# Preparing raw float64 weights in pairs of units instead of one by one

## The chip, the cores and the metric

The kernel runs on one core of a Trainium2 chip. The metric is the device time of one execution in microseconds, as the median of three runs: 1222.59 us before the change (1215.45 to 1223.43).

## What is computed

An attention over 4 batches, 12 heads, 448 tokens and 64 channels, whose queries and keys are normalised per row, feeds two MLPs one after the other. All inputs arrive in float64 or float32; here the weights are read as 64-bit words.

```python
q_n, k_n = rmsnorm(q, g_q), rmsnorm(k, g_k)
attn = softmax(scale * q_n @ k_n.T)          # per batch and head
x = (attn @ v) -> [1792, 768]
x = (x @ w_a) * (x @ w_b) @ w_out            # 768 -> 1536 -> 768
h = x @ w_in                                 # 768 -> 2048
g = np.maximum(h, 0.0) + alpha * np.minimum(h, 0.0)
return g @ w2_out                            # 2048 -> 768
```

## The kernel before

**Stages.** The four batches go through four MLP stages each: `a` (products with w_a and w_b, 24 chains), `y` (w_out of the first MLP, 6 chains in two parts), `h` (w_in of the second, 16 chains) and `o` (w_out of the second, 6 chains in four parts). A hand-written list gives their order: a0 y0 h0 o0 a1 y1 a2 h1 o1 y2 h2 a3 o2 y3 o2 h3 o3. The attention of the next batches is a generator, `att_steps`, of which a few steps are taken at each tick of a stage; the attention of batch 0 runs first, in float32, with nothing to run beside it but the preparation of weights.

**Products.** Each float32 operand is held as a high and a low half in float16, and a product of 128 rows takes three matmuls (`prod`). A *unit* is what one weight tile serves: a chain, or a part of it, of six (a, y, h: 768 columns) or four (o: 512 columns) blocks, so 18 or 12 matmuls of 448 columns. The last o and y stages (o2, y3, o3; `FAST`) use seven formed products for eight, on half the tokens, with weights that `form_weights` combines beforehand from the stored halves through raw buffers and GpSimd's queue.

**Weights.** A list `stream` holds the units in the order of use. The first use of a weight (76 units, all in batch 0's stages) goes through four steps, which `advance` calls as the stream moves on:

- `w_load` (L748): DMA of the 64-bit words into a raw buffer, 12 units ahead of use;
- `w_convert` (L764 to L779), 8 ahead: a Prelu on ScalarE takes the upper words to float32, VectorE shifts (L767) and ORs the lower bits in (L770), ScalarE squares the result with a sum per row (L778);
- `w_scale`, 6 ahead: a matmul with ones (`total`) adds the sums over the partitions, and three small operations on VectorE (`power`) make a power of two as scale and its inverse. For a and h two chains share one such computation, with a scale for each; y takes two parts, o four;
- `w_split` (L831 to L835), 3 ahead: ScalarE writes the scaled high half, VectorE the residual, and SyncE's queue stores both in HBM.

Later uses of the same weight read the stored halves (L744), 4 units ahead; formed weights are read at L738, one unit further ahead. The pools: raw 5 buffers, wf (float32, and formed weights) 6, wh (halves) 5, each for one unit. Two raw buffers (`early`) serve the attention of batch 0 as its transposed queries and keys until that attention ends. `slot` has 35 buffers for activations: X, AB, Y and G. `tmp` has three.

**Order.** The program order gives priorities, and a list scheduler with a cost estimate orders each engine's instructions at build time; where the code says `keep_in_program_order`, that is fixed. Each engine then runs its list in order and waits on semaphores. A stage calls `next_w` (and so `advance`) between a unit's matmuls and the evacuation of its result. SyncE's queue takes in one line the loads of q, k, v and weights, the stores of halves and results, and the transposes of q, k and the probabilities (L355, L358, L490).

Of the kernel before, what the change touches and what calls it, by code (L numbers as in the profile page):

```python
# [19 lines left out]
def attention_gated_mlps_kernel(  # L20
# [24 lines left out]
    SLOTS = 35  # L45
# [25 lines left out]
    def slot32(name):  # L71
# [6 lines left out]
    kd0 = keep_p.tile([128, 2 * KB * D], F32, name="kd0")  # L78
# [15 lines left out]
    cgf = const.tile([128, KF2], F32, name="cgf")  # L94
# [8 lines left out]
        "a": const.tile([128, 2 * KF], F32, name="inv_a"),  # L103
        "y": const.tile([128, KD], F32, name="inv_y"),
        "h": const.tile([128, KF2], F32, name="inv_h"),
# [165 lines left out]
    def prep2f(g):  # L271
        d = P[g]
        kr, r = d["kr"], d["rk"]
        kd = kd0[:KP]
        d["kd"] = kd
        i = nc.vector.tensor_tensor(
            kd.rearrange("p (i h d) -> p h i d", i=KB, h=2),
            kr.rearrange("p (h i) d -> p h i d", h=2),
            r[:KP, NI:NS].rearrange("p (h i) -> p h i", h=2).unsqueeze(3).to_broadcast([KP, 2, KB, D]),
            op=ALU.mult,  # L280
        )
        if g == 0:
            tc.keep_in_program_order(i)
# [379 lines left out]
    def form_block(kind, i, j, cols):  # L663
# [3 lines left out]
        def raw():  # L667
            return raw_p.tile([128, 784], I64, tag="raw", name="raw")

        def load():  # L670
            d["x"] = x = raw().bitcast(F16)[:, 0:8 * w].rearrange("p (q l n) -> p q l n", q=4, l=2)
# [5 lines left out]
        def whole(q):  # L677
            if q == 0:
                d["r"] = raw().bitcast(F32)[:, 0:4 * w].rearrange("p (q n) -> p q n", q=4)
# [45 lines left out]

    def size(kind):
        return CHAINS[kind][2] * 128

    def w_load(u):
# [3 lines left out]
        if key[-1] == "s":  # L733
            kind, i, (f, j), _ = key
            t = wf_p.tile([128, 768], F32, tag="wf", name="ws").bitcast(F16)
            t = t[:, 0:2 * WIDE[kind]].rearrange("p (l n) -> p l n", l=2)
            tc.keep_in_program_order(
                nc.sync.dma_start(out=t, in_=form_source(kind, i, f, j))  # L738
            )
            w16[u] = t  # L740
            return
        if key in scratch:
            t = wh_p.tile([128, 2, 768], F16, tag="w16", name="w16")[:, :, 0:n]
            nc.sync.dma_start(out=t, in_=scratch[key])  # L744
            w16[u] = t
# [3 lines left out]
        if state["pin"]:  # L749
            tc.keep_in_program_order(i)  # L750
        raws[u] = t
        scratch[key] = hbm.tile([128, 2, n], F16, name=f"sc_{key[0]}{key[1]}_{key[2]}")

    def w_convert(u):
# [6 lines left out]
        t = wf_p.tile([128, 768], F32, tag="wf", name="wf")[:, 0:size(kind)]  # L761
# [12 lines left out]
        _, parts, _ = CHAINS[kind]  # L774
        j = (n * parts + part) % (parts * GROUP[kind])
        if j == 0:
            sums[0] = sm_p.tile([128, 4], F32, tag="ss", name="ss")
# [3 lines left out]
        if j == parts * GROUP[kind] - 1:  # L781
            squares[u] = sums[0][:, 0:j + 1]
# [3 lines left out]
    def w_scale(u):  # L786
# [4 lines left out]
        _, parts, _ = CHAINS[kind]  # L791
        chains = GROUP[kind]
        us = range(u - parts * chains + 1, u + 1)
        sc = sm_p.tile([128, 2], F32, tag="sc", name="sc")[:, 0:chains]
        iv = inv[kind][:, n - chains + 1:n + 1]
        power(total(squares.pop(u), len(us), chains), sc, iv, 2)
        for x in us:
            scales[x] = sc[:, (x - us[0]) // parts:(x - us[0]) // parts + 1]
        if (kind, n) == ("h", KF2 - 1):
# [22 lines left out]
    def junk(width, n):  # L822
        return jk_p.tile([128, width], BF16, tag="junk", name="junk")[:, 0:n]

    def w_split(u):
        if u not in scales:
            return
        t, s = wf.pop(u), scales.pop(u)
        n = t.shape[1]
        w = wh_p.tile([128, 2, 768], F16, tag="w16", name="w16")[:, :, 0:n]  # L830
# [5 lines left out]
        w16[u] = w  # L836


    STEPS = [(w_load, 12), (w_convert, 8), (w_scale, 6), (w_split, 3)]
# [4 lines left out]
    again = sorted(set(range(len(stream))) - set(firsts))  # L844
# [96 lines left out]

    def blocks():
        r = raw_p.tile([128, 784], I64, tag="raw", name="raw").bitcast(F32)
        r = r.rearrange("p (j n) -> p j n", j=7)
# [119 lines left out]
    def stage_a(b):  # L1064
        raw = {}
        for f in range(KF):
            for w in range(2):
                yield
                ps = new_ps()[:, 0:S]
                hw = unit()  # L1070
# [292 lines left out]
```

## Time and profile before

| | |
|---|---|
| median of three runs | 1222.59 us (1215.45, 1222.59, 1223.43) |
| profiled execution | 1215.08 us, span 1213.0 us |
| TensorE busy (matmul) | 1145.4 us, 94% |
| VectorE busy | 816.5 us, 67% |
| ScalarE busy | 770.1 us, 63% |
| mean granted TensorE clock | 0.98 |

The shares are means over stages with different limits: the attention of batch 0 and the preparation of weights lie in the first 440 us, while from 440 us on the weights come ready from HBM. Busy times by stretch say more. TensorE's busy time is modelled from pipelined matmuls; its idle time and what ended it are the better guide.

### The profile page before, as it was taken

Reading aid. Unit: us, or ns where it says so; the run is one execution under the profiler, and the core shown is the slowest. Engines: PE = TensorE matmul, PEld = TensorE weight load, DVE = VectorE, ACT = ScalarE, POOL = GpSimd, SP = SyncE. Lnnn points to the kernel's source line nnn. Section 1 sums busy time; section 2 is a strip of 40 time slices with the busy share of each in tenths; the row PEclk is TensorE's granted clock in tenths of the full one; section 3 lists DMA queues with packets and bytes.
Section 4 is the critical chain, followed back from the end, with each engine's and each line's share of the span. In section 5 each row is a group of like instructions: output and inputs, shape, how many; then the busy total and the mean of one; then the engine's idle time right before and its main releaser. Section 6 shows DMA issues by size and latency. Waiting matters only on the chain. (4 is left out here: it accounts for less than half of the span.)

```text
span 1213.0 us, 20078 instructions
## 1 busy us (share of the span) xinstructions
PE 1145.4 (94%) x7144; PEld 650.6 (54%) x7144; DVE 816.5 (67%) x1695; ACT 770.1 (63%) x1543; POOL 108.2 (9%) x176
## 2 busy tenths in 40 slices
PE   6997999899989799998999999999999999999997
PEld 3553554445434344444445554544555558996597
DVE  7898999999899666677754376554356677523631
ACT  7998999999899666767534366564255335513532
POOL 1000000000001000000012100122200562000000
PEclk9997999999989899998999999999999999999999
DMA  7658999999999999987985677898834798873465
GB/s 190 174 163 211 315 326 329 288 298 305 309 246 308 252 237 253 248 199 173 198 225 152 159 175 164 199 222 190 228 117 135 247 299 284 272 210 107 129 188 171
DMA packets 319267, 269.78 MB, mean 222 GB/s; under 512 B 178464, under 2 KB 275232, under 8 KB 319168
## 3 DMA queue, kind: packets, MB, share of 16 engines
q1 hardware_dynamic: 311376, 246.41, 75.9%
q0 software_dynamic: 7792, 22.10, 6.3%
q8 instruction: 56, 0.92, 0.3%
q14 instruction: 43, 0.35, 0.1%
HBM read 179.77 MB, written 43.25 MB: 184 GB/s over the span
## 5 line engine op out<-in xcount | busy, mean ns | idle before, releaser
L110 PEld LDWEIGHTS <-w 128*128 128x128 f16 x4104 | 398.2, 99 | 393.5 <-issue 39.6
L110 PE MATMUL p<-x,w 128*128 128x448 f16 x1728 | 336.3, 354 | 0.5 <-DVE ab L1080 0.4
L110 PE MATMUL p<-y,w 128*128 128x448 f16 x1152 | 221.6, 352 | 1.4 <-DVE t L1187 1.3
L110 PEld LDWEIGHTS <-ws 128*128 128x128 f16 x1386 | 132.5, 98 | 3.3 <-DMA ws<-f_o_S 2.7
L110 PE MATMUL p<-ab,w 128*128 128x448 f16 x648 | 129.7, 359 | 1.3 <-ACT ab L894 1.2
L110 PE MATMUL p<-g,w 128*128 128x448 f16 x576 | 119.8, 362 | 4.6 <-ACT g L1172 3.5
L421 DVE TENSOR_REDUCE nm<-s 128x2 f32<-128x896 f32 x84 | 91.2, 1086 | 33.5 <-PE s L110 33.3
L483 ACT ACTIVATE p<-pf,ri 128x448 f16<-128x448 f32 x126 | 81.8, 665 | 35.9 <-DMA pT<-p 27.4
L484 DVE SCALAR_TENSOR_TENSOR p<-pf,ri,p 128x448 f16<-128x448 f32 x126 | 84.6, 680 | 28.1 <-ACT p L483 28.0
L110 PE MATMUL l<-g,ws 128*128 128x224 f16 x960 | 94.2, 259 | 1.8 <-DMA ws<-f_o_S 1.8
L438 ACT ACTIVATE pf<-s,nm,esc 128x448 f32<-128x448 f32 x126 | 90.0, 719 | 1.4
L832 DVE SCALAR_TENSOR_TENSOR w<-wf,sc,w 128x768 f16<-128x768 f32 (+1 forms) x76 | 70.1, 929 | 2.5 <-ACT w L831 2.1
L831 ACT ACTIVATE w<-wf,sc 128x768 f16<-128x768 f32 (+1 forms) x76 | 65.4, 869 | 2.6 <-DMA sc_h<-w 1.7
L764 ACT ACTIVATE wf<-raw 128x768 f32<-128x768 f32 (+1 forms) x76 | 63.6, 843 | 5.2 <-DMA raw<-in_moe_w_out_dram 3.2
L770 DVE SCALAR_TENSOR_TENSOR wf<-raw,wf 128x768 int32<-128x768 int32 (+1 forms) x76 | 65.7, 868 | 0.3
L1083 ACT ACTIVATE junk<-ab 128x448 bf16<-128x448 f32 x48 | 27.6, 574 | 59.8 <-DVE ab L1080 59.6
L778 ACT ACTIVATE junk<-wf 128x768 bf16<-128x768 f32 (+1 forms) x76 | 59.3, 781 | 1.3 <-DVE wf L770 1.3
L707 POOL DMA_DIRECT2D f_o_S<-raw x48 | 33.8, 807 | 292.6 <-DVE raw L703 214.0
L110 PE MATMUL s<-kT,qT 128*64 128x448 f16 x252 | 48.3, 375 | 11.6 <-DMA kT<-k 9.1
L1080 DVE SCALAR_TENSOR_TENSOR ab<-p,inv_a,t 128x448 f32<-128x448 f32 x48 | 32.5, 678 | 29.6 <-PE p L110 29.0
L110 PE MATMUL s<-early 128*128 128x448 f32 x84 | 39.6, 598 | 10.0 <-ACT pf L438 9.0
L110 PE MATMUL s<-kT,qS 128*64 128x448 f16 x252 | 46.7, 365 | 2.4 <-DMA qS<-qT 2.4
(171 smaller groups left out, 1434.1 us busy)
## 6 DMA issues: line engine op xcount, KB each, us to landing
w<-sc_a SPq DMA_DIRECT2D x72, 384.0 KB, 3.7
w<-sc_h SPq DMA_DIRECT2D x48, 384.0 KB, 3.1
raw<-in_moe_w_in_dram SPq DMA_DIRECT2D x16, 768.0 KB, 7.3
raw<-in_moe_w_out_dram SPq DMA_DIRECT2D x24, 512.0 KB, 6.1
ws<-f_o_S SPq DMA_DIRECT2D x48, 256.0 KB, 3.8
raw<-in_moe_w_a_dram SPq DMA_DIRECT2D x12, 768.0 KB, 7.3
raw<-in_moe_w_b_dram SPq DMA_DIRECT2D x12, 768.0 KB, 6.5
sc_a<-w SPq DMA_DIRECT2D x24, 384.0 KB, 7.3
```

The lines of the kernel that those rows point to most:

```text
L110: nc.tensor.matmul(out=o, lhsT=a, rhs=b, start=first, stop=last)
L421: nc.vector.tensor_reduce(out=nm, in_=ps[:, :, 0:S], axis=AX.X, op=ALU.max, negate=True)
L438: nc.scalar.activation(out=pf, in_=ps[:, j, 0:S], func=AF.Exp, bias=nm[:, j:j + 1], scale=scale[j], accum_out=su[:, j:j + 1],)
L483: nc.scalar.activation(out=t[:, 0, :, 0:KP], in_=pf, func=AF.Copy, scale=r)
L484: nc.vector.scalar_tensor_tensor(out=t[:, 1, :, 0:KP], in0=pf, scalar=r, in1=t[:, 0, :, 0:KP], op0=ALU.mult, op1=ALU.subtract,)
L707: nc.gpsimd.dma_start(out=formed[kind, i, name, j][:, :, cols], in_=d["x"][:, q])
L764: nc.scalar.activation(out=t, in_=hi.bitcast(F32), func=AF.Prelu, scale=2.0 ** -112, alpha=-(2.0 ** 32))
L770: nc.vector.scalar_tensor_tensor(out=ti, in0=lo, scalar=29, in1=ti, op0=ALU.logical_shift_right, op1=ALU.bitwise_or)
L778: nc.scalar.activation(out=junk(768, size(kind)), in_=t, func=AF.Square, accum_out=sums[0][:, j:j + 1])
L831: nc.scalar.activation(out=w[:, 0], in_=t, func=AF.Copy, scale=s)
L832: nc.vector.scalar_tensor_tensor(out=w[:, 1], in0=t, scalar=s, in1=w[:, 0], op0=ALU.mult, op1=ALU.subtract)
L1080: nc.vector.scalar_tensor_tensor(out=ab, in0=ps, scalar=i, in1=t, op0=ALU.mult, op1=ALU.mult)
```

## The change

Two units that follow each other are prepared as one pair. For a the order of the chains becomes a0 a1 b0 b1, so that a pair holds two chains of the same matrix; for h a pair is two chains, for y and o two parts of one chain. A pair has one raw buffer (filled by two DMAs), one Prelu, one shift, one OR, one Square, one scale, one split copy, one residual and one store. Chains of a and h in a pair share their scale, so `inv` and `cgf` have half as many columns; o adds the sums of two pairs. Later uses read a pair with one DMA. Formed weights get pairs of buffers too, by turns from wf and wh, with a DMA for each unit. Pools hold pairs: raw 3, wf 3, wh 3; slot goes from 35 to 33. Raw loads run 11 ahead, and 13 once the first attention is through. `kd`, a buffer of its own before, shares the one of `k16`. `early` is one raw pair. The thrown-away output of the squares is uint8 and not bfloat16. `form_block` takes both its buffers from one raw pair, and `blocks` uses the halves of one by turns. In stage a two results for w_a are held in `tmp` until those for w_b arrive.

```diff
-    SLOTS = 35
+    SLOTS = 33
-    raw_p = ctx.enter_context(tc.tile_pool(name="raw", bufs=5))
+    raw_p = ctx.enter_context(tc.tile_pool(name="raw", bufs=3))
-    wf_p = ctx.enter_context(tc.tile_pool(name="wf", bufs=6))
-    wh_p = ctx.enter_context(tc.tile_pool(name="wh", bufs=5))
+    wf_p = ctx.enter_context(tc.tile_pool(name="wf", bufs=3))
+    wh_p = ctx.enter_context(tc.tile_pool(name="wh", bufs=3))
...
-    early = [raw_p.tile([128, 784], I64, tag="raw", name=f"early{i}").bitcast(F32) for i in range(2)]
+    early = raw_p.tile([128, 2, 784], I64, tag="raw", name="early").bitcast(F32)
+    early = [early[:, i] for i in range(2)]
...
-        kd = kd0[:KP]
-        d["kd"] = kd
+        d["kd"] = kd = one_p.tile([KP, 2 * KB * D], F32, tag="k16", name="kd")
...
-            "a": ((w_a, w_b)[n % 2], n // 2), "y": (w_out, n), "h": (w2_in, n), "o": (w2_out, n)
+            "a": ((w_a, w_b)[n // 2 % 2], n // 4 * 2 + n % 2), "y": (w_out, n), "h": (w2_in, n), "o": (w2_out, n)
...
+    members, apart = {}, [0]
+    for u, key in enumerate(stream):
+        if key[-1] != "s":
+            apart[0] = 0
+            if key[0] in "ah" and key[1] % 2 or key[0] in "yo" and PARTS[CHAINS[key[0]][1]].index(key[2]) % 2:
+                members[u - 1].append(u)
+            else:
+                members[u] = [u]
...
     def w_load(u):
...
         if key[-1] == "s":
...
+            alternate[0] ^= 1
+            if alternate[0]:
+                t = wf_p.tile([128, 2 * 768], F32, tag="wf", name="ws").bitcast(F16)
+                t = t.rearrange("p (u n) -> p u n", u=2)
+            else:
+                t = w_half().rearrange("p u l n -> p u (l n)")
...
         if key in scratch:
-            t = wh_p.tile([128, 2, 768], F16, tag="w16", name="w16")[:, :, 0:n]
-            nc.sync.dma_start(out=t, in_=scratch[key])
-            w16[u] = t
+            t = views(w_half(), n)
+            nc.sync.dma_start(out=t, in_=whole[key])
+            for j, x in enumerate(members[u]):
+                w16[x] = t[:, j]
             return
-        t = raw_p.tile([128, 784], I64, tag="raw", name="raw")[:, 0:n]
-        i = nc.sync.dma_start(out=t.rearrange("p (k f) -> p k f", f=128), in_=source(*key))
...
+        t = raw_p.tile([128, 2 * 784], I64, tag="raw", name="raw")[:, 0:2 * n]
+        whole[key] = hbm.tile([128, 2, 2, n], F16, name=f"sc_{key[0]}{key[1]}_{key[2]}")
+        for j, x in enumerate(members[u]):
+            i = nc.sync.dma_start(
+                out=t[:, j * n:(j + 1) * n].rearrange("p (k f) -> p k f", f=128), in_=source(*stream[x])
+            )
...
     def w_convert(u):
...
-        t = wf_p.tile([128, 768], F32, tag="wf", name="wf")[:, 0:size(kind)]
+        t = wf_p.tile([128, 2 * 768], F32, tag="wf", name="wf")[:, 0:2 * size(kind)]
...
         nc.scalar.activation(
-            out=junk(768, size(kind)), in_=t, func=AF.Square, accum_out=sums[0][:, j:j + 1]
-        )
+            out=junk(1536, 2 * size(kind)), in_=t, func=AF.Square, accum_out=sums[0][:, j:j + 1]
+        )
...
     def w_scale(u):
...
-        sc = sm_p.tile([128, 2], F32, tag="sc", name="sc")[:, 0:chains]
-        iv = inv[kind][:, n - chains + 1:n + 1]
-        power(total(squares.pop(u), len(us), chains), sc, iv, 2)
+        sq = squares.pop(u)
+        us = [u - 2, u][2 - sq.shape[1]:]
+        m = n // 2 if kind in "ah" else n
+        sc = sm_p.tile([128, 1], F32, tag="sc", name="sc")
+        power(total(sq, len(us)), sc, inv[kind][:, m:m + 1], 2)
...
     def w_split(u):
...
-        nc.scalar.activation(out=w[:, 0], in_=t, func=AF.Copy, scale=s)
+        nc.scalar.activation(out=w[:, :, 0], in_=t, func=AF.Copy, scale=s)
         nc.vector.scalar_tensor_tensor(
-            out=w[:, 1], in0=t, scalar=s, in1=w[:, 0], op0=ALU.mult, op1=ALU.subtract
-        )
-        nc.sync.dma_start(out=scratch[stream[u]], in_=w)
+            out=w[:, :, 1], in0=t, scalar=s, in1=w[:, :, 0], op0=ALU.mult, op1=ALU.subtract
+        )
+        nc.sync.dma_start(out=whole[stream[u]], in_=w)
...
-    STEPS = [(w_load, 12), (w_convert, 8), (w_scale, 6), (w_split, 3)]
+    STEPS = [(w_load, 11), (w_convert, 8), (w_scale, 6), (w_split, 3)]
...
-                    if x > u + ahead + (stream[x][-1] == "s") or (f is w_split and x not in scales):
+                    extra = 2 * (stream[x][-1] == "s" or f is w_load and steps is STEPS and not state["pin"])
+                    if x > u + ahead + extra or (f is w_split and x not in scales):
...
     def stage_a(b):
...
-        for f in range(KF):
-            for w in range(2):
+        for n in range(2 * KF):
+            yield
+            f, w = n // 4 * 2 + n % 2, n // 2 % 2
...
```

## Rows read from the trace of the kernel before

**Rows 1.** Busy time in stretches: length, each engine's busy us (instructions), clock, DMA, GB/s.
```profile
core 0: us, PE busy (x) PEld busy (x) DVE busy (x) ACT busy (x) POOL busy (x), PEclk, DMA share, GB/s
...
25.00:105.00 80.00, 68.47 (x418) 39.17 (x418) 72.59 (x213) 77.51 (x177) 0.00 (x0) 0.98 0.60 180
105.00:220.00 115.00, 106.27 (x596) 56.20 (x597) 106.55 (x222) 110.38 (x221) 0.95 (x1) 0.95 1.09 307
220.00:345.00 125.00, 115.29 (x649) 58.13 (x648) 115.40 (x234) 115.52 (x226) 2.38 (x4) 0.98 1.10 302
345.00:440.00 95.00, 81.77 (x453) 39.01 (x452) 72.18 (x166) 77.60 (x168) 5.77 (x8) 0.91 1.07 264
440.00:635.00 195.00, 189.53 (x1112) 92.23 (x1111) 133.94 (x292) 120.69 (x271) 5.22 (x10) 0.98 0.93 216
635.00:1020.00 385.00, 384.02 (x2194) 199.88 (x2194) 219.34 (x372) 178.55 (x340) 88.67 (x138) 1.00 0.73 199
1020.00:1213.00 193.00, 184.89 (x1631) 156.72 (x1628) 79.22 (x138) 73.50 (x111) 0.00 (x0) 0.99 0.59 180
```
**Rows 2.** Waits of TensorE: who waited for whom, us in total, times, longest.
```profile
PE s L110 <- ACT pf L438: 10.7, 10, 4.2
PE s L110 <- DMA kT<-k: 9.1, 4, 5.4
```
**Rows 3.** Groups by line and shape: count, busy us, mean ns; idle before them.
```profile
L764 ACT ACTIVATE wf<-raw 128x768 f32<-128x768 f32 x52 | 47.5, 920 | 2.0 <-DMA raw<-in_moe_w_in_dram 1.7 <-DVE w L832 0.3
L764 ACT ACTIVATE wf<-raw 128x512 f32<-128x512 f32 x24 | 16.1, 678 | 3.2 <-DMA raw<-in_moe_w_out_dram 3.2
L778 ACT ACTIVATE junk<-wf 128x768 bf16<-128x768 f32 x52 | 44.1, 847 | 1.3 <-DVE wf L770 1.3
L778 ACT ACTIVATE junk<-wf 128x512 bf16<-128x512 f32 x24 | 15.3, 636 | 0.0
L831 ACT ACTIVATE w<-wf,sc 128x768 f16<-128x768 f32 x52 | 48.7, 939 | 2.6 <-DMA sc_h<-w 1.7 <-PE p L110 0.8
L831 ACT ACTIVATE w<-wf,sc 128x512 f16<-128x512 f32 x24 | 16.6, 718 | 0.0
L770 DVE SCALAR_TENSOR_TENSOR wf<-raw,wf 128x768 int32<-128x768 int32 x52 | 49.4, 953 | 0.3
L770 DVE SCALAR_TENSOR_TENSOR wf<-raw,wf 128x512 int32<-128x512 int32 x24 | 16.3, 685 | 0.0
L832 DVE SCALAR_TENSOR_TENSOR w<-wf,sc,w 128x768 f16<-128x768 f32 x52 | 52.6, 1013 | 1.7 <-ACT w L831 1.3
L832 DVE SCALAR_TENSOR_TENSOR w<-wf,sc,w 128x512 f16<-128x512 f32 x24 | 17.5, 747 | 0.8 <-ACT w L831 0.8
```
**Rows 4.** Timeline of ScalarE and VectorE near 370 us: start, us, instruction.
```profile
369.31 1.32 ACT L831 ACTIVATE w<-wf,sc 128x512 f16<-128x512 f32 x2
...
371.10 1.23 ACT L764 ACTIVATE wf<-raw 128x512 f32<-128x512 f32 x2
...
374.25 0.64 ACT L778 ACTIVATE junk<-wf 128x512 bf16<-128x512 f32 x1
374.79 0.19 ACT L778 ACTIVATION_READ_ACCUMULATOR junk<-wf 128x1 f32 x1
374.87 0.72 ACT L831 ACTIVATE w<-wf,sc 128x512 f16<-128x512 f32 x1
...
370.16 1.41 DVE L832 SCALAR_TENSOR_TENSOR w<-wf,sc,w 128x512 f16<-128x512 f32 x2
...
372.75 1.29 DVE L770 SCALAR_TENSOR_TENSOR wf<-raw,wf 128x512 int32<-128x512 int32 x2
```
**Rows 5.** Stretches for line L764 alone: ScalarE's busy time and instructions in it.
```profile
25.00:105.00 80.00, 7.46 (x8) 0.98 0.60 180
```
**Rows 6.** Timeline of SyncE's queue: the issue of one store.
```profile
388.73 0.54 SPq L835 DMA_DIRECT2D sc_o<-w  x1
```
**Rows 7.** DMA issues of the page: count, KB each, median us to landing.
```profile
w<-sc_a SPq DMA_DIRECT2D x72, 384.0 KB, 3.7
```
**Rows 8.** Timeline of TensorE: the longest of four waits for formed weights.
```profile
1039.28 7.07 PE L110 MATMUL l<-g,ws 128*128 128x224 f16 x72 [0.62 <-DMA ws<-f_o_S]
```

More of the change, by code (lines that the diff above doesn't have):

```diff
@@ L678, in whole @@
             if q == 0:
-                d["r"] = raw().bitcast(F32)[:, 0:4 * w].rearrange("p (q n) -> p q n", q=4)
+                d["r"] = d.pop("t").bitcast(F32)[:, 0:4 * w].rearrange("p (q n) -> p q n", q=4)
             q = slice(q, q + 2)
@@ L773, in w_convert @@
         wf[u] = t
-        _, parts, _ = CHAINS[kind]
-        j = (n * parts + part) % (parts * GROUP[kind])
+        pairs = 2 if kind == "o" else 1
+        j = PARTS[4].index(part) // 2 if kind == "o" else 0
         if j == 0:
-            sums[0] = sm_p.tile([128, 4], F32, tag="ss", name="ss")
+            sums[0] = sm_p.tile([128, 2], F32, tag="ss", name="ss")
         nc.scalar.activation(
-            out=junk(768, size(kind)), in_=t, func=AF.Square, accum_out=sums[0][:, j:j + 1]
+            out=junk(1536, 2 * size(kind)), in_=t, func=AF.Square, accum_out=sums[0][:, j:j + 1]
         )
-        if j == parts * GROUP[kind] - 1:
-            squares[u] = sums[0][:, 0:j + 1]
+        if j == pairs - 1:
+            squares[u] = sums[0][:, 0:pairs]
     sums, squares = [None], {}
@@ L843, in attention_gated_mlps_kernel @@
     firsts = [u for u, key in enumerate(stream) if key[-1] != "s" and not (key in seen or seen.add(key))]
-    again = sorted(set(range(len(stream))) - set(firsts))
+    firsts = [u for u in firsts if u in members]
+    again = sorted(x for x in set(members) - set(firsts))
     at = [[0] * len(STEPS), [0] * len(AGAIN)]
@@ L940, in form_steps @@
             f += [x[:, :, j] for j in range(j1 - j0)]
+    other = []
     def blocks():
-        r = raw_p.tile([128, 784], I64, tag="raw", name="raw").bitcast(F32)
-        r = r.rearrange("p (j n) -> p j n", j=7)
+        if not other:
+            r = raw_p.tile([128, 2, 784], I64, tag="raw", name="raw").bitcast(F32)
+            other.extend([r[:, 1], r[:, 0]])
+        r = other.pop().rearrange("p (j n) -> p j n", j=7)
         return r, (r[:, 0:3:2], r[:, 3:5])
@@ L1065, in stage_a @@
         raw = {}
-        for f in range(KF):
-            for w in range(2):
-                yield
-                ps = new_ps()[:, 0:S]
-                hw = unit()
-                for c in range(KD):
-                    prod(ps, hw, c, X[b, c], c == 0, c == KD - 1)
-                i = inv["a"][:, 2 * f + w:2 * f + w + 1]
-                next_w()
-                if w == 0:
-                    t = tmp()
-                    nc.scalar.activation(out=t, in_=ps, func=AF.Copy, scale=i)
-                else:
-                    raw[f] = ab = slot32(f"ab32_{b}_{f}")
-                    nc.vector.scalar_tensor_tensor(
-                        out=ab, in0=ps, scalar=i, in1=t, op0=ALU.mult, op1=ALU.mult
-                    )
-                    nc.scalar.activation(
-                        out=junk(768, S), in_=ab, func=AF.Square,
-                        accum_out=ssab[:, b % 2, f:f + 1],
-                    )
+        t = {}
+        for n in range(2 * KF):
+            yield
+            f, w = n // 4 * 2 + n % 2, n // 2 % 2
+            ps = new_ps()[:, 0:S]
+            hw = unit()
+            for c in range(KD):
+                prod(ps, hw, c, X[b, c], c == 0, c == KD - 1)
+            i = inv["a"][:, n // 2:n // 2 + 1]
+            next_w()
+            if w == 0:
+                t[f] = tmp()
+                nc.scalar.activation(out=t[f], in_=ps, func=AF.Copy, scale=i)
+            else:
+                raw[f] = ab = slot32(f"ab32_{b}_{f}")
+                nc.vector.scalar_tensor_tensor(
+                    out=ab, in0=ps, scalar=i, in1=t.pop(f), op0=ALU.mult, op1=ALU.mult
+                )
+                nc.scalar.activation(
+                    out=junk(1536, S), in_=ab, func=AF.Square,
+                    accum_out=ssab[:, b % 2, f:f + 1],
+                )
         for kk in range(KD):
@@ L1165, in one @@
                 nc.scalar.activation(
-                    out=rs[i][1][j], in_=halves_of(t), func=AF.Copy, scale=cgf[:, f:f + 1]
+                    out=rs[i][1][j], in_=halves_of(t), func=AF.Copy, scale=cgf[:, f // 2:f // 2 + 1]
                 )
```

63 lines of the change are left out of this document (36 added, 27 removed).

## Prediction
> **What bounds the kernel now.** I read first the busy time by stretch [rows 1]. From 635 to 1020 us TensorE is busy for 384.02 of 385 us: nothing that ScalarE or VectorE saves there can shorten the run. From 440 to 635 and from 1020 to the end it is idle for 5.5 and 8.1 us. The rest of its idle time lies before 440 us: 11.5 us in 25 to 105, 8.7 in 105 to 220, 9.7 in 220 to 345 and 13.2 in 345 to 440. That is just where the raw weights are prepared. ScalarE is at 77.51 of 80 us and at 110.38 of 115 us in the first two stretches, so it is the bound of the first and close to a second bound in the next two; VectorE stands at about 92% in both of these. In 345 to 440 (stage o0) neither is full, 77.60 and 72.18 of 95 us, and yet TensorE waits most there.
>
> Then the waits of TensorE [rows 2]: its two largest sums are scores that wait for the exponential (10.7 us) and for a transposed key (9.1 us over four waits, one of 5.4). The first is ScalarE's backlog. The second runs through SyncE's queue, which issues the transposes of keys, queries and probabilities in one line with all weight loads and stores.
>
> The granted clock was 0.95, 0.98 and 0.91 in the three stretches from 105 to 440 us [rows 1], which costs about 5.8 + 2.5 + 8.6 = 16.8 us of TensorE time, an estimate from clock and length; idle time there sums to 31.7 us. So one us of idle time goes together with 0.53 us of lost clock.
>
> **The change part by part.** *Merged operations.* 76 units become 38 pairs. Two back-to-back operations of 512 columns against one of 1024, whose length I extend from the two forms that the trace has [rows 3], with the steps of [rows 4]:
> - Prelu (L764): 1.23 us for two; one of 1024 is 0.678 + 2 x (0.920 - 0.678) = 1.162. Saves 0.07.
> - Square with its accumulator read (L778): 374.25 to 374.87 is 0.62 a unit, 1.24 for two. One Square adds 2 x (0.847 - 0.636) = 0.42 to that 0.62, 1.04. Saves 0.20.
> - Split copy (L831): 1.32 against 0.718 + 2 x 0.221 = 1.160. Saves 0.16.
> - On VectorE the OR (L770): 1.29 against 1.221, 0.07; the residual (L832): 1.41 against 1.279, 0.13; the shift (L767) I take like the OR, 0.07.
>
> A pair saves 0.43 us on ScalarE and 0.27 on VectorE; the 768 forms have the same fixed part, since I fit one line through both. For 38 pairs that is 16.3 and 10.3 us. 8 units are converted in 25 to 105 us [rows 5], so 4 pairs, whose conversion and Square give 4 x 0.27 = 1.1 us where ScalarE is the bound: **minus 1.1**. The other 15.2 us fall after 105 us. Their worth lies between nothing (TensorE was busy while they ran, and only the backlog shrinks) and 15.2 us (all of it stood in the way). With 31.7 us idle and two engines above 92% until 345 us, I take half: **minus 7.6**. Lost clock goes with it at 0.53: **minus 4.0**.
>
> The Trainium skill, in "Perfetto Trace Analysis", section "Optimizing Scalar/DVE Operations", puts the fixed cost of an operation in SBUF at about 93 ns on ScalarE and about 60 ns on VectorE. By it the pairs save 38 x 3 x 0.093 = 10.6 us on ScalarE, not 16.3, half of its late part is 4.8, and the end would be some 4 us later than mine. I stay with the rows, which hold the accumulator read too.
>
> *SyncE's queue.* 38 stores are left out at 0.54 us each [rows 6], 20.5 us of its issue time. The loads of raw weights stay 76. A store of a pair waits for a longer split (about 1.8 us against 1.01), and transposes queue behind it. The worth is between nothing and the 9.1 us of the key waits; I take a quarter of that, **minus 2**, since only the longest of the four stands beside a full queue.
>
> *Reloads.* Later batches read a pair with one DMA. A unit's reload lands in 3.7 us [rows 7]; twice that is 7.4. The load of a pair finds its buffer free when the pair three back is done, so four units lie ahead of its use. 2194 matmuls in 385 us are 0.175 us each, 3.2 us for a unit of 18, so 12.6 us of TensorE work hide it. Nothing. Without this cover a late reload would cost up to 7.4 us at a stage's start.
>
> *Formed weights of the fast stages.* Their units come in pairs from two pools of three buffers: up to 12 units ahead instead of 6. TensorE waits for them four times, at most 0.62 us [rows 8]. **Minus 1.**
>
> *Buffers.* The raw, f32 and f16 pools hold 6, 6 and 6 units instead of 5, 6 and 5, though in whole pairs. Raw loads run 13 units ahead after the first attention instead of 12, conversion stays 8 ahead, so the DMA has more time. At the first attention `early` takes one of three raw pairs, leaving 4 units instead of 3. `kd` shares a buffer with `k16`, as short-lived as before. Nothing.
>
> *Slots, 35 to 33.* By the code the most are live at the end of h1: 6 of Y, 12 of AB, 2 of X and the growing G. With 33 the last three G wait for Y, that is for the last matmul of h1; the three `tmp` buffers hold them meanwhile. They are then split one after another: three of at most 0.72 us and one trailing 0.75 [rows 3], 2.9 us, and o1 reads the first of them only in its third unit. Between nothing and 3 us; I take nothing, as o1's first two units are the cover.
>
> *Order a0 a1 b0 b1, one scale per pair.* As many scale computations as before, one column narrower; the sum over columns falls away for y. Two `tmp` are held, of three. Nothing.
>
> *Coarser grain.* A split copy of 1536 columns is 0.939 + 3 x 0.221 = 1.60 us, 0.66 longer than now, and an exponential or an evacuation that becomes ready behind it waits longer. In 25 to 105 us there are about 12 such operations on ScalarE: 12 x 0.66 = 8 us if each stands in front of a round, none if the round was queued anyway, which ScalarE's 97% speaks for. After that, three PSUM buffers hide an evacuation late by 0.66 us. I take **plus 3**.
>
> **Sum:** -1.1 - 7.6 - 4.0 - 2 - 1 + 3 = -12.7 us. The profiled execution took 1215.1 us (span 1213.0, 2.1 around it), so its like would take 1202. It was as fast as the fastest timed run (1215.45); the median is 1222.6, and the saving from there gives 1210 us.
>
> **The rivals.** *Hidden:* the savings fall where TensorE is busy, and the transitions are set by other chains (AB's sum of squares, the transposes). Only the first stretch and the formed weights give something: 1222.6 - 2.1 = 1220.5. For it speaks that 31.7 idle us are spread over many small waits; against it, that ScalarE is full right up to the ends of a0 and h0.
>
> *Grain, slower:* longer operations stand in front of what TensorE waits for. The place is 25 to 440 us: 8 us as above, and of the 102 long operations on ScalarE after 105 us one in ten by 0.66 us, 6.7, together 14.7 less 1.1, so 1236. It decides from about that tenth on, if nothing of the relief arrives. Stage o0 speaks for it, where TensorE waits beside engines that aren't full; the saturation before 345 us speaks against it. The same section of the Trainium skill has both sides: grouping helps a saturated engine, while engines that are not saturated but cause bubbles elsewhere are better served by operations broken up. By that rule o0 loses and the stretches before it win. The traces so far agree with its first half only as far as the fullness goes; no run here shows the second half.
>
> *Full relief:* all 15.2 us arrive, with clock: -1.1 - 15.2 - 8.1 - 2 - 1 = -27, 1195 us.
>
> *Slots:* the pairs give nothing and h1's end costs 3 us: 1225.
>
> **Chances.** The forecast, with its own range 1199 to 1219, 0.55; hidden 0.22; grain 0.12; full relief 0.08; slots 0.03. About 1% is what a measurement of this kernel tells from no change, so faster means below 1210.4 and slower above 1234.8. Of the forecast 0.33 lies below 1210.4: faster 0.33 + 0.08 = 0.41. Slower: 0.09 of grain. Same: the rest, 0.50. From 1197 to 1230 leaves out most of full relief and of grain and the edges, about 0.2.
>
> **What would show it.** Right: ScalarE's busy time falls by some 16 us and VectorE's by 10; TensorE's idle time in 105 to 440 us falls from 31.7 to near 24 and its clock there rises; the key waits shrink; from 635 us on the trace is as it was. Hidden: the same busy times, idle time as before. Grain: more waits of scores for exponentials, longer idle at the ends of a0, h0 and in o0. Slots: idle time of TensorE at the start of o1. Most likely to make me wrong is the half that I took between two far ends, and that a changed order of instructions shifts the chance waits, such as the 5.4 us for a key, either way.

## The result and the profile after

The changed kernel takes 1224.83 us as the median of 20 runs (1219.22 to 1230.31), the kernel before 1215.32 us (1211.56 to 1228.66) beside it: a ratio of 1.0073, 95% interval 1.0055 to 1.0090. The forecast was a gain of 12.7 us, counted from the earlier median of 1222.6 us to 1210; it is a loss of 9.5 us. The profiled execution of the changed kernel has a span of 1228.5 us and is the longest of its 20, so its stage times stand a few us high.

Busy time in stretches after, with the columns of [rows 1]:

```profile
core 0: us, PE busy (x) PEld busy (x) DVE busy (x) ACT busy (x) POOL busy (x), PEclk, DMA share, GB/s
25.00:105.00 80.00, 65.75 (x398) 37.99 (x397) 68.27 (x200) 74.90 (x155) 0.00 (x0) 0.96 0.54 176
105.00:220.00 115.00, 109.13 (x595) 57.09 (x595) 101.86 (x175) 103.59 (x169) 0.00 (x0) 0.96 0.95 292
220.00:345.00 125.00, 115.49 (x646) 59.84 (x645) 110.12 (x196) 107.31 (x169) 2.33 (x5) 0.96 1.04 290
345.00:440.00 95.00, 80.77 (x471) 40.16 (x468) 75.05 (x144) 79.07 (x142) 5.77 (x8) 0.96 1.06 286
440.00:635.00 195.00, 175.59 (x1038) 86.35 (x1039) 125.28 (x266) 117.81 (x265) 1.21 (x4) 0.98 0.92 204
```

ScalarE and VectorE are relieved as forecast: over the whole span ScalarE is busy for 755.9 us against 770.1, VectorE for 805.6 against 816.5. TensorE did not turn that into time. Worse, it lost most where the change removes nothing: in 440 to 635 us it is busy for 175.59 us, against 189.53 in [rows 1].

The merged operations on pairs of 768 columns, to be held against [rows 3]: count, busy us, mean ns, idle time before them.

```profile
L798 ACT ACTIVATE wf<-raw 128x1536 f32<-128x1536 f32 x26 | 41.9, 1611 | 8.4 <-DMA raw<-in_moe_w_in_dram 5.0 <-DVE w L866 1.2 <-DVE sab L120 1.1
L812 ACT ACTIVATE junk<-wf 128x1536 uint8<-128x1536 f32 x26 | 38.7, 1488 | 6.0 <-DVE wf L804 4.9 <-DVE pw L117 1.0
L865 ACT ACTIVATE w<-wf,sc 128x1536 f16<-128x1536 f32 x26 | 40.8, 1571 | 0.0
L866 DVE SCALAR_TENSOR_TENSOR w<-wf,sc,w 128x1536 f16<-128x1536 f32 x26 | 47.2, 1815 | 6.2 <-ACT w L865 6.1
```

A split copy of a pair takes 1.57 us against two of 0.94, close to the 1.60 worked out. But ScalarE now stands idle for 8.4 us ahead of these conversions, 5.0 of them for raw words of `w_in`, where it stood 2.0, 1.7 of them for such words.

Waits of TensorE after, to be held against [rows 2]:

```profile
PE s L110 <- ACT pf L437: 13.0, 13, 2.5
PE p L110 <- DVE ab L1122: 6.9, 5, 2.3
PE x L110 <- DVE pw L117: 6.8, 2, 4.0
PE s L110 <- DMA kT<-k: 4.0, 4, 1.9
```

Key waits fell from 9.1 to 4.0 us, as hoped, while others grew or came: for the product AB (0.4 us before) and for a scale.

**By stage.** Taken from the timeline of TensorE, from the first matmul of a stage to that of the next:

| | start of a0 | a0 to h0 | o0 | a1 | y1 to the end |
|---|---|---|---|---|---|
| before | 115.9 | 221.1 | 101.0 | 115.3 | 659.7 |
| changed | 121.9 | 225.9 | 93.2 | 129.7 | 657.8 |

So o0 gained 8 us, the stages behind a1 gained 2; the first attention lost 6, a0 to h0 lost 5, and a1 lost 14. In a1 no raw weight is loaded, converted or split; what the change does there is to reload a pair by one DMA.

Waits of ScalarE and VectorE in a1, the kernel before (who waited for whom, us in total, times, longest):

```profile
ACT sk L236 <- DMA kr<-in_k_dram: 4.8, 3, 2.6
DVE stat L240 <- ACT sk L236: 4.4, 4, 2.4
```

The same two in the changed kernel:

```profile
ACT sk L236 <- DMA kr<-in_k_dram: 12.6, 4, 6.1
DVE stat L240 <- ACT sk L236: 20.4, 5, 7.6
```

Both engines run their lists in order. They stand until a load of keys has landed; what is behind them in the list comes late, and in a1 TensorE waits 5.6 us for `ab`, for which it didn't wait there before. That the one follows from the other is argued; the experiments come back to it. The timelines of SyncE's queue and of ScalarE show one such place:

```profile
488.69 0.42 SPq L206 DMA_DIRECT2D kr<-in_k_dram  x1
...
495.31 0.63 ACT L236 ACTIVATE sk<-kr 112x512 f32<-112x512 f32 x1 [6.13 <-DMA kr<-in_k_dram]
```

The attention takes two heads at a time; these pairs of heads (not the pairs of weights) are counted from 0 to 23, six a batch, so pair 17 is the last of batch 2. The load above, that for pair 17, is issued at 488.69; ScalarE has stood for 6.13 us when it can take the squares of these keys at 495.31.

### The profile page after: what moved, and what is told of

Read it like the earlier page. It is cut to its first block, busy times and chain, and to the rows that moved or that the text cites. A ratio compares the mean times of both kernels' runs of the same rounds, so it can differ in the third digit from the quotient of the medians.

```text
span 1228.5 us, 19435 instructions
## 1 busy us (share of the span) xinstructions
PE 1145.9 (93%) x7144; PEld 655.4 (53%) x7144; DVE 805.6 (66%) x1575; ACT 755.9 (62%) x1391; POOL 114.4 (9%) x176
## 5 line engine op out<-in xcount | busy, mean ns | idle before, releaser
L110 PEld LDWEIGHTS <-w 128*128 128x128 f16 x4776 | 462.3, 99 | 406.6 <-issue 51.9
L110 PE MATMUL p<-g,w 128*128 128x448 f16 (+1 forms) x588 | 119.4, 357 | 4.2 <-DVE g L1215 1.7
L482 ACT ACTIVATE p<-pf,ri 128x448 f16<-128x448 f32 x126 | 81.3, 663 | 46.8 <-DMA pT<-p 37.5
L110 PEld LDWEIGHTS <-ws 128*128 128x128 f16 x714 | 68.5, 98 | 0.4
L866 DVE SCALAR_TENSOR_TENSOR w<-wf,sc,w 128x1536 f16<-128x1536 f32 (+1 forms) x38 | 62.6, 1646 | 8.8 <-ACT w L865 8.7
L798 ACT ACTIVATE wf<-raw 128x1536 f32<-128x1536 f32 (+1 forms) x38 | 55.7, 1465 | 12.3 <-DMA raw<-in_moe_w_in_dram 5.0
L804 DVE SCALAR_TENSOR_TENSOR wf<-raw,wf 128x1536 int32<-128x1536 int32 (+1 forms) x38 | 60.3, 1586 | 0.2
L812 ACT ACTIVATE junk<-wf 128x1536 uint8<-128x1536 f32 (+1 forms) x38 | 51.4, 1353 | 7.5 <-DVE wf L804 6.3
L110 PE MATMUL x<-pT,v 112*64 112x448 f16 x432 | 47.5, 372 | 8.2 <-DVE pw L117 6.8
L865 ACT ACTIVATE w<-wf,sc 128x1536 f16<-128x1536 f32 (+1 forms) x38 | 54.5, 1434 | 0.4 <-DMA sc_o<-w 0.4
L110 PE MATMUL s<-early 128*128 128x448 f32 x84 | 41.6, 624 | 10.9 <-ACT pf L437 7.7
L110 PE MATMUL l<-g,ws 128*128 128x224 f16 x480 | 49.6, 259 | 0.0
```

What stands on the lines that cost most here:

```text
L110: nc.tensor.matmul(out=o, lhsT=a, rhs=b, start=first, stop=last)
L482: nc.scalar.activation(out=t[:, 0, :, 0:KP], in_=pf, func=AF.Copy, scale=r)
L798: nc.scalar.activation(out=t, in_=hi.bitcast(F32), func=AF.Prelu, scale=2.0 ** -112, alpha=-(2.0 ** 32))
L804: nc.vector.scalar_tensor_tensor(out=ti, in0=lo, scalar=29, in1=ti, op0=ALU.logical_shift_right, op1=ALU.bitwise_or)
L812: nc.scalar.activation(out=junk(1536, 2 * size(kind)), in_=t, func=AF.Square, accum_out=sums[0][:, j:j + 1])
L865: nc.scalar.activation(out=w[:, :, 0], in_=t, func=AF.Copy, scale=s)
```

## Experiments

All ratios are to the kernel before, run beside it on the same chip. "Transposes" in the table below counts, in SyncE's queue as the trace shows it, the transposes of probabilities ahead of the load of keys for pair 17 and, behind the comma, for pair 18; "gap" is the time between the loads for pairs 16 and 17. The recorded expectations are one off here: the 49, 56, 62 or 63 that they give for the loads of pairs 16 and 17 stand in the traces ahead of those of pairs 17 and 18. All stages are in us, from one profiled execution each, which for e4, e5 and e9 is the fastest of the run and for e10, e15, e16 and the changed kernel the slowest; a few us between two rows say little.

| | ratio | transposes | gap | start of a0 | a0 to h0 | o0 | a1 |
|---|---|---|---|---|---|---|---|
| before | 1 | 49, 56 | 9 | 115.9 | 221.1 | 101.0 | 115.3 |
| e2 | 1.0014 | 49, 56 | 10 | 115.5 | 219.3 | 98.8 | 117.5 |
| e5 | 0.9999 | 49, 56 | 8 | 116.1 | 218.8 | 99.3 | 114.8 |
| e6 | 1.0003 | 49, 56 | 8 | 115.8 | 221.6 | 100.6 | 115.2 |
| e8 | 0.9962 | 49, 56 | 5 | 123.5 | 218.8 | 91.3 | 119.3 |
| e9 | 0.9976 | 49, 56 | 6 | 121.0 | 218.9 | 89.0 | 117.7 |
| e11 | 1.0045 | 49, 56 | 5 | 123.2 | 225.2 | 97.1 | 117.5 |
| e16 | 0.9966 | 49, 56 | 4 | 118.6 | 226.5 | 90.8 | 117.9 |
| e18 | 0.9953 | 49, 56 | 2 | 117.7 | 225.1 | 89.3 | 116.6 |
| e15 | 1.0096 | 49, 56 | 11 | 116.5 | 224.2 | 99.1 | 122.7 |
| e13 | 1.0150 | 54, 56 | 18 | 126.0 | 220.2 | 100.7 | 125.4 |
| e17 | 1.0004 | 56, 62 | 19 | 114.4 | 228.3 | 90.6 | 121.8 |
| e14 | 1.0064 | 56, 63 | 19 | 115.8 | 222.2 | 94.2 | 121.9 |
| e7 | 1.0052 | 56, 63 | 22 | 121.1 | 225.2 | 89.5 | 125.0 |
| e10 | 1.0142 | 54, 63 | 21 | 115.6 | 222.0 | 99.0 | 125.3 |
| e4 | 1.0088 | 54, 62 | 18 | 111.8 | 225.8 | 93.0 | 125.7 |
| e1 | 1.0175 | 54, 62 | 17 | 119.4 | 231.5 | 93.2 | 128.7 |
| e12 | 1.0016 | 56, 63 | 23 | 118.4 | 219.8 | 87.8 | 129.1 |
| e3 | 1.0068 | 56, 62 | 29 | 113.8 | 231.7 | 89.4 | 129.6 |
| changed | 1.0073 | 56, 63 | 23 | 121.9 | 225.9 | 93.2 | 129.7 |

**Order of chains and grain (e1 to e4).** e1 takes the changed kernel back to the order a0 b0 a1 b1, e2 gives the new order to the kernel before, e3 and e4 split the operations on pairs into one per unit, during the first attention or throughout.

```diff
-            "a": ((w_a, w_b)[n // 2 % 2], n // 4 * 2 + n % 2), "y" ...
+            "a": ((w_a, w_b)[n % 2], n // 2), "y" ...
...
-        nc.scalar.activation(out=w[:, :, 0], in_=t, func=AF.Copy, scale=s)
+        for c in [slice(0, 1), slice(1, 2)] ...:
+            nc.scalar.activation(out=w[:, c, 0], in_=t[:, c], func=AF.Copy, scale=s)
```

> The changed kernel with one part undone: the chains of a run a0 b0 a1 b1 again, so a pair holds one chain of w_a and the matching one of w_b. Theory 'order': the 14 us that stage a1 lost (115 to 130 us) come from two results for w_a and then two for w_b being evacuated on one engine each; a1 goes back to some 115 us and the run to about 0.989 of the changed kernel, 0.996 of the kernel before. Rival 'slots' (33 instead of 35 buffers for activations, or pairs being reloaded late): a1 stays near 130 us and the ratio to before near 1.007.

> The kernel before with one part of the change alone: the order a0 a1 b0 b1 in the stream and in stage a, weights still prepared one by one, 35 slots. 'Order': a1 grows by 10 to 14 us and the run is 1.008 to 1.012 of the kernel before. 'Slots' or late pairs: no difference, 1.000.

> The changed kernel, but during the first attention (batch 0) each of the Prelu, shift, OR, Square, split copy and residual works on one unit again, two operations per pair; buffers, transfers and scales stay pairs. Theory 'grain': the first float16 scores, 6.9 us later than before the change (113.6 against 106.7), come back to about 107, and the run gains some 5 us (0.996 of the changed kernel, 1.003 of before). Rival 'buffers' (two raw pairs beside early, kd in the buffer of k16, SyncE's queue held up by a load of v): they stay at 113 or later, since the merged operations' saving of about 1.5 us is gone too.

> The changed kernel with every pair's operations split in two throughout, pairs kept only for buffers, transfers and scales. If the 8 us that o0 gained came from ScalarE's and VectorE's saved fixed cost, o0 goes back from 93 to about 101 us and the run is slower than with fine operations in the first attention alone, by some 5 to 8 us. If o0 gained by fewer stores in SyncE's queue, o0 stays near 93 us. ScalarE's busy time goes back up by about 14 us either way.

Measured: e1 1.0175 (1.0126 to 1.0224), e2 1.0014 (0.9993 to 1.0036), e3 1.0068 (1.0044 to 1.0092), e4 1.0088 (1.0057 to 1.0119). The order of chains isn't the cause: e2 shows nothing, and e1 is slower still, by 1% and with a1 at 128.7 us; why, wasn't found. Nor is the grain, either way: with every operation split again the kernel is, within the intervals, no faster and no slower than the changed one, and o0 is as short (93.0 us). The profiles of e3 and e4 do start a0 8 and 10 us earlier than the changed kernel's, but merged kernels (e12, e16 to e18) start it 3 to 8 us earlier too, and by o0 e3 has lost most of it again.

**Slots and reloads (e5 to e7), raw loads (e8).** e5 is the kernel before with 33 slots; e6 the kernel before with two reloads issued at once; e7 the changed kernel with a reload for each unit; e8 as e7, with a raw load for each unit at its own time as well.

```diff
-            nc.sync.dma_start(out=t, in_=whole[key])
+            nc.sync.dma_start(out=w16[u], in_=scratch[key])
...
-        for j, x in enumerate(members[u]):
-            i = nc.sync.dma_start(... source(*stream[x]))
+        i = nc.sync.dma_start(... source(*key))
```

> The kernel before with 33 slots instead of 35 and nothing else. Slots theory: the buffers for activations are what holds a1 up; then stage a1 grows from 115 us towards the 130 us of the changed kernel, and the ratio to the kernel before is about 1.007 or more. Bulk theory (the reload of a pair is one DMA of twice the size in front of the attention's loads and transposes): slots do nothing in a1, which stays at 115 to 118 us, and the ratio is 1.000 within 0.003.

> The kernel before, with the second reload of each two that follow each other issued together with the first, one unit of work earlier than before; all else as before, operations unit by unit, buffers unit by unit. Bulk theory: two reloads at once stand in front of the attention's loads and transposes, which land later; a1 grows from 115 us by 5 to 14 us, idle time of TensorE in it from 5 us to 10 or more, and the ratio to the kernel before is 1.004 to 1.012. If the bulk of the reloads is not the cause: a1 stays at 115 to 118 us and the ratio is 1.000 within 0.003.

> The changed kernel, with the later batches' reloads as one DMA of 384 KB for each unit, each issued at its own unit's time, into its half of the pair buffer; all else as changed. Bulk theory: a1 comes back from 130 us to 115 to 119 us, TensorE's idle time there from 18.6 us to below 9, and the run is some 10 us shorter than the changed kernel, about 0.998 of the kernel before. If the bulk is not the cause: a1 stays at 127 to 131 us and the ratio at 1.005 to 1.009.

> As the run with reloads by unit, and the raw float64 weights too are loaded unit by unit, each at its own time, instead of two DMAs at once. Bulk theory for the first attention: the first score for a key of the next batch comes back from 113.6 us towards 107 us, as in the kernel before, and the run is another 3 to 6 us shorter, about 0.994 of the kernel before. If the first attention's loss has another cause (two raw pairs beside the early buffers instead of three units, kd in a shared buffer): that time stays at 111 to 114 us, and the ratio is that of the run with reloads by unit.

Measured: e5 0.9999 (0.9975 to 1.0022), e6 1.0003 (0.9984 to 1.0021), e7 1.0052 (1.0034 to 1.0071), e8 0.9962 (0.9945 to 0.9980). Slots cost nothing. The theory that the reloads' bulk does the harm fell: e6 shows none, and e7 mends little. Raw loads one by one are worth 0.9%, about 10 us between the medians of e7 and e8, and make of the loss a small gain. The first score for a key of the next batch came at 106.3 us in e8 (106.7 before, 113.6 changed), as its theory had it, but a0 starts no earlier for it (123.5 us).

**Raw loads alone (e9 to e12).** e9 is the changed kernel with raw loads unit by unit and reloads in pairs; e11 and e12 do the same only during the first attention, or only after it. e10 is the kernel before, with the first raw load of each two held back for the second:

```diff
+                    late = f is w_load and steps is STEPS and not second[x]
-                    if x > u + ahead + (stream[x][-1] == "s") or ...
+                    if x + late > u + ahead + (stream[x][-1] == "s") or ...
```

> The changed kernel with the raw float64 weights loaded unit by unit, each at its own time (one DMA of 768 KB) instead of two DMAs at once; reloads stay one DMA for a pair. Raw-bulk theory (two raw loads at once are what the change lost): the run is as that with all loads by unit, 0.996 of the kernel before, first attention's end near 107 us. If the reloads' bulk costs as well: 0.998 to 1.000. If only both together help: 1.005.

> The kernel before, where the first raw load of each two waits one unit of work for the second, so that both are issued at once as in the changed kernel; nothing else changed, all operations unit by unit. Raw-bulk theory: slower, ratio to the kernel before 1.005 to 1.01, and the first score for a key of the next batch goes from 107 us to 110 us or more. If bulk hurts only with pairs of buffers (two pairs are all that is free in the first attention) or by the order that follows from it: 1.000 within 0.003.

> The changed kernel with raw loads unit by unit during the first attention alone, two at once from then on. If the loss is made in the first attention: the first score for a key comes at 106 to 108 us instead of 113.6, and the ratio is 0.996 to 1.000. If it is made later, beside the stages: the first attention is shorter but the ratio stays at 1.004 or more.

> The reverse: raw loads two at once in the first attention, unit by unit from then on. If the loss is made in the first attention: first score for a key at 111 to 114 us and a ratio of 1.004 to 1.008. If it is made later: 0.998 to 1.001, with the first attention as long as in the changed kernel and stage a1 near 119 us.

Measured: e9 0.9976 (0.9958 to 0.9994), e10 1.0142 (1.0113 to 1.0172), e11 1.0045 (1.0024 to 1.0066), e12 1.0016 (0.9994 to 1.0038). With raw loads two at once the loss is there in both kernels, with one by one it isn't. An early first score doesn't mend it: e11 has it at 105.4 us and still loses, with a0 no earlier (123.2). Nor is a1 all of it: e11 loses with a short a1 (117.5 us), while e12, with a long one (129.1), has no loss that its interval shows. And e10 did not behave as its theory said: up to a1 it is as fast as the kernel before (a1 begins at 436.6 us, there at 438.0). It loses 10 us in a1 and 8.6 in y2, where no raw load is left. What a raw load changes there should be the order of instructions, which the build's scheduler writes from an estimate that runs through the whole program. The table shows that the order does change: the load of keys for pair 17 stands behind 49 transposes in some kernels, behind 54 or 56 in the others. With 49, a1 takes 115 to 119 us in all but e15; with 54 or 56, 122 to 130.

**The order itself (e13 to e17), and a better version (e16, e18).** e14 and e17 move one line that has nothing to do with weights, the sums of squares of the values ("value norms"), in the kernel before and in e16; e13 and e15 write the loads of q and k a step earlier in the changed kernel and in e10; e16 is the changed kernel with raw pairs 12 units ahead; e18 is e16 with a reload for each unit.

```diff
 e14, e17
-                    if c == (6 if g % 2 or g < NP else 1) and g + NP < B * NP:
+                    if c == (6) and g + NP < B * NP:
 e13 (e15: only for g >= NP)
-                    if c == 5:
+                    if c == (4):
                         load_qk(g + 3)
 e16
-    STEPS = [(w_load, 11), (w_convert, 8), (w_scale, 6), (w_split, 3)]
+    STEPS = [(w_load, 12), (w_convert, 8), (w_scale, 6), (w_split, 3)]
```

> The changed kernel with the loads of q and k for the third pair ahead written one step of the attention earlier (at its step 4 instead of 5); raw loads stay two at once. In SyncE's queue the load of keys for pair 17 then stands behind 56 transposes of probabilities instead of 63. Order theory: a1 falls from 130 us to 115 to 120 us, and the run to 0.997 to 1.002 of the kernel before. Bulk theory (two raw loads at once do the harm by themselves): a1 stays at 125 us or more and the ratio at 1.004 to 1.009.

> The kernel before with one line moved: the value norms of the even pairs from the seventh on are written at step 6 of the attention instead of step 1. No load of weights is touched, but in SyncE's queue the load of keys for pair 17 then stands behind 63 transposes of probabilities instead of 56, as in the changed kernel. Order theory: a1 grows from 115 us to 125 to 130 us and the ratio is 1.005 to 1.012. Bulk theory: a1 stays at 115 to 119 us, ratio 1.000 within 0.003.

> The kernel before with two raw loads at once (that run alone: 1.0142), and the loads of q and k of the later batches written at step 4 of the attention instead of 5, which brings the load of keys for pair 17 from behind 63 transposes of probabilities back to 56. Order theory: a1 returns from 125 us to 115 to 119 us, and the ratio falls by some 0.008 to 1.003 to 1.008. Bulk theory: a1 stays at 125 us, ratio 1.012 to 1.016.

> The changed kernel with raw pairs loaded 12 units ahead instead of 11, still two loads at once; the order built from it has the load of keys for pair 17 behind 56 transposes of probabilities. Order theory: a1 at 115 to 120 us, and the run 0.996 to 1.002 of the kernel before. Bulk theory: as the changed kernel, 1.004 to 1.009, a1 at 125 us or more.

> The changed kernel with raw pairs loaded 12 units ahead (0.9966 of the kernel before), and the value norms of the even pairs from the seventh on written at step 6 of the attention instead of 1. In the order built from it the load of keys for pair 16 stands behind 56 transposes of probabilities instead of 49, that for pair 17 behind 62 instead of 56. Order theory: a1 grows from 118 us to 124 to 130 us, and the ratio from 0.9966 to 1.002 to 1.008. If the order in a1 does not matter by itself: a1 stays at 118 us, ratio 0.995 to 0.999.

> The changed kernel with raw pairs loaded 12 units ahead and, in addition, the later batches' reloads as one DMA of 384 KB for each unit at its own time instead of one of 768 KB for a pair. If reloads of pairs cost something by themselves: 0.992 to 0.995. If they cost nothing once the order is good: 0.9966 within 0.002.

Measured: e13 1.0150 (1.0127 to 1.0173), e14 1.0064 (1.0047 to 1.0082), e15 1.0096 (1.0080 to 1.0112), e16 0.9966 (0.9951 to 0.9980), e17 1.0004 (0.9983 to 1.0024), e18 0.9953 (0.9930 to 0.9975).

The loads of keys for pairs 16 to 18 as SyncE's queue issued them, from its timeline in the kernel before:

```profile
455.78 0.58 SPq L206 DMA_DIRECT2D kr<-in_k_dram  x1
464.63 0.58 SPq L206 DMA_DIRECT2D kr<-in_k_dram  x1
483.71 0.31 SPq L206 DMA_DIRECT2D kr<-in_k_dram  x1
```

In e14, the kernel before with the value norms moved:

```profile
459.20 0.44 SPq L206 DMA_DIRECT2D kr<-in_k_dram  x1
478.48 0.60 SPq L206 DMA_DIRECT2D kr<-in_k_dram  x1
506.54 0.95 SPq L206 DMA_DIRECT2D kr<-in_k_dram  x1
```

In e16, the changed kernel with raw pairs 12 units ahead:

```profile
449.18 0.62 SPq L206 DMA_DIRECT2D kr<-in_k_dram  x1
453.47 0.38 SPq L206 DMA_DIRECT2D kr<-in_k_dram  x1
477.99 0.39 SPq L206 DMA_DIRECT2D kr<-in_k_dram  x1
```

In e17, which is e16 with the value norms moved:

```profile
458.28 0.57 SPq L206 DMA_DIRECT2D kr<-in_k_dram  x1
477.61 0.58 SPq L206 DMA_DIRECT2D kr<-in_k_dram  x1
503.67 0.57 SPq L206 DMA_DIRECT2D kr<-in_k_dram  x1
```

e14 and e17 put the second of these loads 19 us behind the first instead of 9 and 4, and the third 23 us later in the one and 26 in the other. Neither edit touches a weight. a1 grows by 6.6 and 3.9 us, the run by 0.64% and, between the ratios of e17 and e16, by 0.38%. The ratio of e14 is where the order theory had it; a1 in both (121.9 and 121.8 us) and the ratio of e17 lie between the two theories. In e14 ScalarE's waits for keys in a1 are close to those of the changed kernel:

```profile
ACT sk L236 <- DMA kr<-in_k_dram: 12.0, 4, 5.6
DVE stat L240 <- ACT sk L236: 12.5, 4, 6.6
```

In the other direction e16 keeps two raw loads at once, changes one number, has the early order, and a1 is back at 117.9 us, the run at 0.9966, both as the order theory had it. So for a1 the order is a cause by itself, and two raw loads at once are none. That it acts through the one load of keys isn't shown. ScalarE's waits for keys don't follow the length of a1: in e16 they come to 9.1 us with a short a1, while e4 and e10 have a1 at 125 us with waits of 5.6 and 6.0 us. In e16:

```profile
ACT sk L236 <- DMA kr<-in_k_dram: 9.1, 4, 4.2
```

e15 brings the load for pair 17 back to 49 transposes, yet a1 falls only from 125.3 to 122.7 us, less than the order theory asked for, and its ratio of 1.0096 fits neither theory; y2 is back at 46.8 us. e13 didn't put the theory to the test that it was meant for: its edit moved the load for pair 18 from behind 63 to behind 56 transposes, that for pair 17 only from 56 to 54, and a1 stays long (125.4). Its ratio of 1.0150 is above both theories; it loses also in the first attention and in o0, for reasons not found. And the kernels with the late order that were not made so by the value norms have 125 to 130 us in a1, 3 to 8 more than e14 and e17: the rest of that order differs as well, and what of it costs these us wasn't told apart.

e18 is the fastest: 1208.28 us beside 1213.71, faster than both kernels. Its distance to e16 is within the intervals, so a price of reloads in pairs stays unproved.

## Why the prediction was wrong

**Busy times: right.** ScalarE fell by 14.2 us (16.3 worked out), VectorE by 10.9 (10.3).

**Half of the relief after 105 us, minus 7.6, and its clock, minus 4.0: wrong.** This is the largest term, and it isn't there. TensorE's idle time in the stretches from 105 to 440 us fell from 31.7 to 29.6 us, not to 24. a0 to h0, the stretches with full engines, became longer (221.1 to 225.9), and e4, which gives back all of the merging on ScalarE and VectorE, runs like the changed kernel within the intervals. Relief of a full engine was read as time, but these stages stood nearly full on TensorE as well. The windows of a0 to h0, before and after:

```profile
115.90:337.00 221.10, 209.71 (x1195) 107.64 (x1193) 205.55 (x421) 208.61 (x410) 3.32 (x5) 0.99 1.10 311
121.90:347.80 225.90, 213.57 (x1197) 111.18 (x1195) 199.80 (x343) 197.94 (x310) 2.33 (x5) 0.97 1.02 299
```

TensorE is idle for 11.4 us of the one and 12.3 of the other. What grew is its busy time, at a granted clock of 0.97 instead of 0.99: about 4.6 us, an estimate from clock and length, nearly the whole 4.8. In these two executions the lost clock didn't go away with idle time, it moved here from o0, below. The step that failed is the chance of a half between two ends, taken without a row that showed TensorE waiting for these operations, and the clock that was hung on it. Of the rivals *hidden* described this best: the busy times as forecast, the idle time nearly as before.

By the Trainium skill, "Perfetto Trace Analysis", section "Optimizing Scalar/DVE Operations", grouping can help a saturated engine, and breaking up may help where unsaturated engines cause bubbles. Neither shows here: a0 to h0 gained nothing from merging, and splitting the operations again left a0 to h0 (225.8 us) and o0 (93.0) as they were (e4).

**SyncE's queue, minus 2: too small.** In o0, which became 7.8 us shorter, the waits for keys shrank. TensorE's waits for `kT` in o0 of the kernel before:

```profile
PE s L110 <- DMA kT<-k: 7.3, 3, 5.4
```

And of the changed kernel:

```profile
PE s L110 <- DMA kT<-k: 1.9, 2, 1.4
```

But these waits are not the whole of it. The windows of o0, before and after:

```profile
337.00:438.00 101.00, 83.52 (x463) 39.64 (x462) 79.12 (x178) 83.97 (x182) 5.77 (x8) 0.92 1.06 261
347.80:441.00 93.20, 78.44 (x458) 39.44 (x457) 72.25 (x141) 77.30 (x138) 5.77 (x8) 0.96 1.06 283
```

TensorE's idle time fell by 2.7 us; 5.1 us are busy time, at a granted clock of 0.96 instead of 0.92. Other kernels show that few key waits don't make a short o0: e13 has 0.9 us of them and 100.7 us. Nearly all kernels with pairs have 88 to 93 us in o0, those with units 94 to 101; e11 and e13 are exceptions. The shorter o0 doesn't come from the merged operations (e4). That it comes from the 38 stores left out is not shown: no run stored by unit and merged the rest.

**Coarser grain, plus 3: nothing that shows** in the ratios of e3 and e4, whose intervals leave room for some 3 us. The rival that was slower by grain, with 25 to 440 us as its place, had the cause and the place wrong: the largest loss is in a1, and splitting doesn't mend it.

**Formed weights, minus 1: fits.** The four waits of [rows 8], 1.8 us together, are gone, and y1 to the end took 1.9 us less.

**Slots, reloads, order of chains at nothing: right** in the kernel before (e5, e6, e2).

**Raw loads at nothing: wrong.** "Raw loads run 13 units ahead after the first attention instead of 12 ..., so the DMA has more time" looked at how far ahead the loads stand and not at what goes out with them. One by one the changed kernel is faster by 0.97% (1.0073 against 0.9976 in e9), and two at once make the kernel before slower by 1.42% (e10). That is mostly not a price of two loads at once, but of the order that came with them: e16 loads two at once, 12 units ahead, and has 0.9966. A part may lie in the stages with raw loads. In the changed kernel ScalarE waits 5.0 us for raw words, in the rows of the merged operations; in e9 and in e16 such waits are not among those that these rows list. With two at once after the first attention, kernels with pairs need 225 to 232 us for a0 to h0 (e13 220.2), with one by one 219 to 220 (e8, e9, e12). But e16 needs 226.5 without those waits, so that difference stays unexplained.

**What the sum left out** is the order that the build writes. The prediction named it last, as "a changed order of instructions shifts the chance waits, such as the 5.4 us for a key, either way". It should have stood among the rivals with a1 as its place. There the changed kernel lost 14 us in its profile (e7, its like, 10), more than the whole sum was to save, with TensorE's idle time up from 5.1 to 18.9 us. e14 shows that such a change of order costs 0.64% with no weight touched, and e16 that the changed kernel with another order gains 0.34%. Of the kernels with pairs and the early order, e8, e9, e16 and e18 gain 0.2 to 0.5%, up to half of the 1% forecast; e11 gains nothing. Which wait carries the order's price in a1 stays open.

The median lies inside the given range, 1197 to 1230. That is luck: for none of the reasons given for its upper part, and with a start of 1222.6 us for a kernel that took 1215.3 beside it.

## What to carry to other kernels

When a build orders instructions by an estimate, any edit can reorder all that follows. Before a small gain or loss is put down to the edit, compare the built order of the busy stages behind it, loads above all, and try a neighbouring setting, as e16 did with one number. Where operations are merged, the loads that feed them can still go one by one: nothing of the gain hung on two at once (e9). Count a saving on a full engine as time only where the bounding engine is seen to wait for it.

## What the runs showed of the hardware

A single load of 224 KB of keys, issued 21 us further into a1 than before (488.69 against 464.63 us, a1 itself 3.0 us later), stopped ScalarE for 6.1 us at one instruction, and VectorE behind it, though both are busy for less than two thirds of that stage (79.9 and 82.1 of 129.7 us).

In e10's y2 TensorE stood for 4.9 us ahead of a product of probabilities with no releaser in the profile, and the stage took 8.6 us more than before (55.5 us). In e15, which moves only loads of queries and keys, it takes 46.8 us again. The cause of the wait itself wasn't found.
